# A gated feed-forward layer on one core: the start-up transposes of x from four transfers instead of two, five constant matmuls, and a weight load of its own

## The chip, the core and the metric

The kernel runs on one core of one Trainium2 chip. A core has a matrix engine (PE, with its weight loads shown apart as PEld), a vector engine (DVE), an activation engine (ACT), a general engine (POOL) and a sync engine (SP); SP and ACT also issue the transfers (DMAs) here, each on a queue of its own, and 16 DMA engines serve both. Every engine runs its own stream of instructions in order, and semaphores tie the streams together. The metric is the time of one execution in device microseconds; several runs of a kernel give a median.

## What is computed

```python
B, S, D, F = 32, 32, 1024, 3584
# x: (B, S, D), w_gate and w_up: (D, F), w_down: (F, D), all bf16
def reference(x, w_gate, w_up, w_down):
    return (_gelu(x @ w_gate) * (x @ w_up)) @ w_down
```

`_gelu` is the tanh approximation. The 32 x 32 tokens are one axis of 1024.

## The kernel before

All of the program is recorded first and emitted afterwards. `pr.add` (line 52) notes an operation with its engine, its output and its inputs; from the tiles that it reads and writes it finds the earlier operations that it must wait for. PE's stream is emitted in the order in which the program text adds the operations. The streams of the other engines are sorted by a due time `at` that is written beside each operation, and by the order of adding where due times agree. `emit` (line 106) puts the waits in front of an operation, and it is the line (117, where the instruction is made) that the profile shows for nearly all instructions; so the rows of the profile are told apart by tiles and shapes.

The tokens are two halves of 512. The first half against the first ten column blocks of the gate and up weights is multiplied in bf16, directly ("raw"); the rest of the first product and the second product use sums of operands (a Strassen-like scheme) in a 32-bit format. The change is in the first microseconds alone, and what matters of the kernel is its start:

- The tile `one` is a constant of ones. Line 200 issues eight matmuls on it, six of 512 and two of 128 columns, into PSUM bank 3. Nothing reads their result.
- The raw products need x transposed, with the contraction axis on the partitions: `xT[0]`, or `x0`, of shape (128, 8, 512), one slice for each 128 columns of x. Slices 2 to 7 come by transposing DMAs (line 215, five issues on SP). Slices 0 and 1 (`NX = 2`) are made by PE: the first 512 tokens' first 256 columns are loaded as they lie in memory into `xn` (128 tokens on the partitions, four token tiles `t`, 256 columns). Token tiles 0 and 1 come with one DMA on SP's queue, 2 and 3 with one on ACT's (line 205), 128 KB each.
- Both DMAs are the first on their queues. Behind them, SP issues four weight loads (gate, 128 KB each) and the transposing DMAs; ACT issues eight weight loads (lines 210 to 218), then loads its activation table and runs a one-element activation into `warm` (line 219). The loads go to `quad[q][:, j, k]`: four column blocks `q` of 512 columns, `j` 0 for gate and 1 for up, and row block `k`.
- Eight transposes on PE (lines 220 to 225) take a 128 x 128 piece each of `xn` with `ident`, an identity that POOL makes. For each slice `k` and each pair of token tiles `i`, two transposes fill a half-bank, and one DVE copy takes it to `xT[0]`. The banks are 6 and 7 for slice 0, and 4 and 5 for slice 1. The order is slice 0 with token tiles 0, 1, 2, 3, then slice 1 likewise.
- The raw matmuls (lines 262 to 267) follow: slice `k`, then matrix `j`, then column block `m`, into bank `2 * m + j`. The first needs both copies of slice 0 and the first gate load. Then come those of the second quad (lines 274 to 287): slices 0 to 5 in the same order, then the last two slices for each column block. The second quad's weights of row blocks 4 to 7 are four ACT loads with due times 9 and 10 (lines 268 to 270), behind ACT's first copies out of PSUM.

In a plain matmul the program gives the stationary operand and the moving operand in one call, and the instruction pair "load weights, multiply" is made of it. `held_matmul` (line 172) makes a multiply alone, on weights that stand in the array already:

```python
        def held_matmul(eng, out, lhsT, rhs, start, stop, skip_group_check=False):
            return eng.add_instruction(mybir.InstMatmult(
                start_tensor_calc=start, stop_tensor_calc=stop, ldweights=False,
```

Of the kernel before, what the change touches and what calls it, by code (L numbers as in the profile page):

```python
# [6 lines left out]
P = 128  # L7
BF16 = mybir.dt.bfloat16
# [115 lines left out]
def bass_standalone__geglu_ffn__sampling_kernel(  # L124
# [10 lines left out]
    _, F = w_gate.shape  # L135
    DK, FM = D // P, F // P
# [3 lines left out]
    x_r = xf.rearrange("(tc p) d -> p tc d", p=P)  # L140
# [3 lines left out]
    pr = _Program()  # L144

    with ExitStack() as es:
        def sb(name, shape, dtype):
            return es.enter_context(nc.sbuf_tensor(name, shape, dtype))
# [7 lines left out]
        ident = sb("ident", [P, P], BF16)  # L156
        warm = sb("warm", [P, 2], FP32)
        p1 = sb("p1", [P, 512], FP32)
        ps = es.enter_context(nc.psum_tensor("ps", [P, 8, 512], FP32))
        const0 = nc.const_aps.tensor(0.0, [P, 1], FP32)  # L160

        xT = [arena[:, a:a + 4096].rearrange("p (k n) -> p k n", n=512) for a in (16384, 0)]
        quad = [arena[:, a:a + 8192].rearrange("p (j k c) -> p j k c", j=2, k=DK) for a in (20480, 8192)]
        def duo(a): return arena[:, a:a + 4096].rearrange("p (j k c) -> p j k c", j=2, k=DK)
        wd = [[arena[:, a:a + 7168].rearrange("p (k n) -> p k n", n=512) for a in row] for row in ((0, 7168), (14336, 21504))]
        xn = hT[:, FM - 1, :].rearrange("p (t c) -> p t c", c=2 * P)
# [12 lines left out]
        def mm(bank, lhsT, rhs, start, stop, held=False, add=False):  # L179
            return pr.add("pe", held_matmul if held else "matmul", ps[:, bank, 0:rhs.shape[-1]], lhsT, rhs,  # L180
                          start=start, stop=stop, skip_group_check=add)
# [4 lines left out]
        def act(out, a, f, at):  # L186
            return pr.add("act", "activation", out, a, f, at=at)

        def dma(eng, out, a, at, name, after=()):
            return pr.add(eng, "dma_start", out, a, at=at, dma=name, after=after)  # L190
# [6 lines left out]
        pr.add("pool", "memset", ident[:, :], 0.0)  # L197
        pr.add("pool", "affine_select", ident[:, :], ident[:, :], [[-1, P]], ALU.not_equal, 1.0,
               base=0, channel_multiplier=1)
        for n in [512] * 6 + [P] * 2:  # L200
            mm(3, one[:, 0:P], one[:, 0:n], True, True)

        NX = 2
        for i, eng in enumerate(("sp", "act")):
            dma(eng, xn[:, 2 * i:2 * i + 2, :], x_r[:, 2 * i:2 * i + 2, 0:NX * P], 0, f"xn{i}")

        def load_quad(eng, q, j, k0, k1, at=0, after=()):
            dma(eng, quad[q][:, j, k0:k1, :], w_r[j][:, k0:k1, 4 * q * P:4 * (q + 1) * P], at, f"w{q}_{j}_{k0}", after)
# [8 lines left out]
            for j in range(2):  # L217
                load_quad("act", 1, j, k, k + 1)
        act(warm[:, 0:1], const0, GELU, 0)
        for k in range(NX):  # L220
            for i, b in enumerate((6, 7) if k == 0 else (4, 5)):
                half = ps[:, b, 0:P].bitcast(BF16)
                for t in range(2):
                    pr.add("pe", "transpose", half[:, t * P:(t + 1) * P], xn[:, 2 * i + t, k * P:(k + 1) * P], ident[:, :])
                pr.add("dve", "tensor_copy", xT[0][:, k, i * 256:(i + 1) * 256], half)

# [15 lines left out]
        bank = lambda b: ps[:, b, :]  # L244
# [7 lines left out]
        x0, x1 = xT  # L252

        def raw(m, j, k, b, start):
            return mm(b, quad[m // 4][:, j, k, m % 4 * P:(m % 4 + 1) * P], x0[:, k, :], start, k in (NX - 1, 3, DK - 1), add=not start and k >= NX)

        def raw_done(m, b, at):
            act(tmp[:, m % 4, :], bank(b), GELU, at)
# [3 lines left out]
        for k in range(NX):  # L262
            for j in range(2):
                for m in range(4):
                    raw(m, j, k, 2 * m + j, k == 0)
                    if k == NX - 1:
                        copy(("act", "dve")[m % 2], kept[m][:, j, :], bank(2 * m + j), 6.5 + 0.9 * j + 0.1 * m)
# [9 lines left out]
        for m, j, k in steps:  # L277
            if j is None:
                raw_done(4 + m, 2 * m, 19.4 + m * 0.87)
                continue  # L280
            begin_late = raw(4 + m, j, k, 2 * m + j, k == 0)
            if k == 3:
                copy(("act", "dve")[m % 2], kept[4 + m][:, j, :], bank(2 * m + j), 14.5)
            if k == 2 and m == j == 0:
                for k0 in range(NX, DK, 2):
                    for i in range(2):
                        load_quad("sp", 0, i, k0, k0 + 2, 9, [begin_late] if k0 == NX and i == 0 else ())


        for m in (0, 2):  # L290
            at = 21.9 + 2.59 * m
            four = [(n, j) for n in (m, m + 1) for j in range(2)]
            for n, j in four:
                copy(("act", "dve")[j], bank(2 * n + j), kept[n][:, j, :], at - 1.5 + 0.8 * (n - m) if m == 0 else at - 2)
            for k0, k1 in ((NX, 4), (4, DK)):
                for n, j in four:
                    for k in range(k0, k1):
                        raw(n, j, k, 2 * n + j, False)
                    if k1 == 4:
                        copy("act", kept[n][:, j, :], bank(2 * n + j), at + 0.6 + 0.43 * (2 * (n - m) + j))  # L300
                    elif j == 1:
                        raw_done(n, 2 * n, at + 2.7 + 1.73 * (n - m))
# [344 lines left out]
```

## Time and profile before

| | us |
|---|---|
| median of 3 runs | 272.19 |
| lowest and highest of them | 271.77, 272.44 |
| span of the profiled execution | 270.8 |
| PE busy in it | 268.2 |
| DVE, ACT, POOL busy in it | 208.2, 136.1, 37.1 |

The span goes from the first to the last instruction of one profiled execution; the time of a run contains some 1.4 us more. Times in the profile are counted from the start of the span. "Issue to landing" of a DMA is the time from its issue on a queue to the last update of its semaphore. The rows of SPq and ACTq are the issues of DMAs, which don't count as busy time of these engines. In the groups and timelines a row reads: start, length, engine, line, operation, out<-in, shape, how many, and in brackets the idle time of the engine before it with what ended it. Issues at the start, by these rows: x on both queues at 0.73 and 0.74 (0.49 and 0.46 us each), weights from 1.25 on, about one each 0.5 us on either queue, the transposing DMAs from 3.17 to 11.51 on SP; the activation table from 5.25 on ACT, for 1.28 us; the first copy out of PSUM on ACT at 7.73.

### The profile page before, as it was taken

What the parts mean: (1) busy time and instruction counts of PE and PEld (TensorE: products, weight loads), DVE (VectorE), ACT (ScalarE), POOL (GpSimd) and SP (SyncE); (2) the same over time, 40 slices, a digit from 0 to 9 for tenths busy, and PEclk for the clock granted to TensorE, in tenths of its full rate; (3) what the DMA queues carried; (4) which work ended last, traced back from release to release, by engine and by line L of the source; (5) the groups of instructions that cost most, each with busy time, mean ns of one, the idle gap of its engine ahead of it and who ended that gap; (6) DMA issues with size and microseconds to landing.
All of it is one profiled execution on the core that took longest, in us unless ns stands there. A gap on an engine that the chain in (4) does not pass through costs nothing.

```text
span 270.8 us, 3333 instructions
## 1 busy us (share of the span) xinstructions
PE 268.2 (99%) x1206; PEld 192.6 (71%) x1206; DVE 208.2 (77%) x246; ACT 136.1 (50%) x221; POOL 37.1 (14%) x23
## 2 busy tenths in 40 slices
PE   8999999999999999999999999999999999999997
PEld 4444448888888888888776776674458888888884
DVE  1338998998899889988764739379976999999921
ACT  2339877566756675667455554531220305057452
POOL 1000003123302330233344160000000000000000
DMA  6999970050492002971900070294010000002102
GB/s 205 205 316 204 280 188 4 13 141 0 116 291 60 0 0 80 254 251 51 263 0 0 0 247 27 65 351 129 0 39 19 4 0 0 0 0 80 58 21 97
DMA packets 45024, 27.47 MB, mean 101 GB/s; under 512 B 8656, under 2 KB 45008, under 8 KB 45008
## 3 DMA queue, kind: packets, MB, share of 16 engines
q1 hardware_dynamic: 42496, 25.04, 34.0%
q10 hardware_dynamic: 2512, 2.23, 3.3%
q8 instruction: 9, 0.15, 0.2%
q14 instruction: 7, 0.06, 0.1%
HBM read 23.33 MB, written 2.10 MB: 94 GB/s over the span
## 4 chain that ended last, share of the span: by engine, by line
PE 99%; DVE 0%; issue 0%
PE ps L117 99%; DVE o L117 0%
## 5 line engine op out<-in xcount | busy, mean ns | idle before, releaser
L117 PE MATMUL ps<-S,T 128*128 128x512 f32 x560 | 129.2, 391 | 0.0
L117 PEld LDWEIGHTS ps<-S,T 128*128 128x128 f32 x560 | 105.2, 188 | 22.3
L117 ACT ACTIVATE tmp<-ps 128x512 f32<-128x512 f32 x64 | 38.0, 596 | 51.7 <-PE ps L117 51.5
L117 POOL TENSOR_TENSOR T<-arena 128x1024 fp32r<-128x1024 bf16 x17 | 36.4, 2153 | 124.5 <-PE ps L117 81.7
L117 PE MATMUL ps<-T,S 128*128 128x512 f32 x224 | 51.3, 390 | 0.0
L117 DVE TENSOR_TENSOR T<-arena,T 128x1024 fp32r<-128x1024 bf16 x42 | 51.0, 1220 | 0.2
L117 PEld LDWEIGHTS ps<-T,S 128*128 128x128 f32 x224 | 42.1, 188 | 8.8
L117 ACT ACTIVATE ps<-ps 128x512 f32<-128x512 f32 x44 | 25.6, 584 | 37.0 <-PE ps L117 37.0
L117 DVE TENSOR_TENSOR hT<-tmp,ps 128x512 bf16<-128x512 f32 x56 | 37.0, 684 | 8.7 <-PE ps L117 6.7
L117 PE MATMUL ps<-arena 128*128 128x512 bf16 x192 | 43.5, 385 | 0.1
L117 DVE TENSOR_TENSOR tmp<-ps,tmp 128x512 f32<-128x512 f32 x28 | 19.4, 692 | 23.5 <-PE ps L117 23.5
L117 PEld LDWEIGHTS ps<-arena 128*128 128x128 bf16 x192 | 18.5, 99 | 23.7 <-issue 2.4
L117 DVE TENSOR_TENSOR T<-arena 128x1024 fp32r<-128x1024 bf16 x25 | 30.0, 1222 | 4.4 <-PE ps L117 4.3
L117 DVE TENSOR_TENSOR ps<-ps,tmp 128x512 f32<-128x512 f32 x32 | 22.3, 696 | 3.0 <-PE ps L117 3.0
L117 PE MATMUL ps<-arena,hT 128*128 128x512 bf16 (+2 forms) x126 | 24.6, 356 | 0.0
L117 PEld LDWEIGHTS ps<-arena,hT 128*128 128x128 bf16 x126 | 11.7, 98 | 12.7 <-issue 0.5
L117 ACT ACTIVATE tmp<-tmp 128x512 f32<-128x512 f32 x28 | 17.6, 632 | 2.4 <-DVE tmp L117 2.1
L117 ACT ACTIVATE ps<-hT 128x512 f32<-128x512 f32 x22 | 13.0, 599 | 7.6 <-DVE hT L117 7.6
L117 DVE TENSOR_TENSOR S<-hT 128x1024 fp32r<-128x1024 bf16 x14 | 16.6, 1221 | 0.0
L117 ACT ACTIVATE T<-arena 128x1024 fp32r<-128x1024 bf16 x14 | 14.8, 1059 | 0.0
L117 ACT ACTIVATE hT<-ps 128x512 f32<-128x512 f32 x18 | 9.5, 602 | 7.0 <-PE ps L117 7.0
L117 PE MATMUL ps<-S 128*128 128x512 f32 x56 | 12.9, 389 | 0.0
(33 smaller groups left out, 94.4 us busy)
## 6 DMA issues: line engine op xcount, KB each, us to landing
arena<-in_w_down_dram SPq DMA_DIRECT2D x4, 1792.0 KB, 9.4
arena<-in_w_gate_dram SPq DMA_DIRECT2D x10, 512.0 KB, 4.8
arena<-in_w_up_dram SPq DMA_DIRECT2D x10, 512.0 KB, 5.9
out_dram<-arena SPq DMA_DIRECT2D x12, 128.0 KB, 1.7
arena<-in_w_up_dram ACTq DMA_DIRECT2D x6, 128.0 KB, 5.6
arena<-in_w_gate_dram SPq DMA_DIRECT2D x3, 256.0 KB, 6.3
arena<-in_w_up_dram SPq DMA_DIRECT2D x3, 256.0 KB, 6.5
arena<-in_w_gate_dram SPq DMA_DIRECT2D x4, 128.0 KB, 5.1
```

Of the source, the lines that this page charges most:

```text
L117: ins = name(eng, *args, **kw) if callable(name) else getattr(eng, name)(*args, **kw)
```

## The change

x's first columns come as four DMAs of one token tile each: tiles 0 and 1 on SP's queue, 2 and 3 on ACT's, each with a semaphore of its own. The eight transposes run in another order, mixed between slices, with a DVE copy as soon as the second transpose of a half-bank is added; banks and copies are the same. Of the eight constant matmuls, five of 512 columns remain. The weights of the first raw matmul are loaded by an instruction of their own, which waits only for the first gate load; the matmul behind it is a held one, which waits for the copies. All other instructions keep their order on every engine.

```diff
-        for n in [512] * 6 + [P] * 2:
+        for n in [512] * 5:
             mm(3, one[:, 0:P], one[:, 0:n], True, True)
 
         NX = 2
         for i, eng in enumerate(("sp", "act")):
-            dma(eng, xn[:, 2 * i:2 * i + 2, :], x_r[:, 2 * i:2 * i + 2, 0:NX * P], 0, f"xn{i}")
+            for t in range(2 * i, 2 * i + 2):
+                dma(eng, xn[:, t, :], x_r[:, t, 0:NX * P], 0, f"xn{t}")
...
-        for k in range(NX):
-            for i, b in enumerate((6, 7) if k == 0 else (4, 5)):
-                half = ps[:, b, 0:P].bitcast(BF16)
-                for t in range(2):
-                    pr.add("pe", "transpose", half[:, t * P:(t + 1) * P], xn[:, 2 * i + t, k * P:(k + 1) * P], ident[:, :])
-                pr.add("dve", "tensor_copy", xT[0][:, k, i * 256:(i + 1) * 256], half)
+        half = {(k, i): ps[:, 6 - 2 * k + i, 0:P].bitcast(BF16) for k in range(NX) for i in range(2)}
+        for t, k in ((0, 0), (0, 1), (2, 0), (1, 0), (2, 1), (3, 0), (1, 1), (3, 1)):
+            i = t // 2
+            pr.add("pe", "transpose", half[k, i][:, t % 2 * P:(t % 2 + 1) * P], xn[:, t, k * P:(k + 1) * P], ident[:, :])
+            if t % 2:
+                pr.add("dve", "tensor_copy", xT[0][:, k, i * 256:(i + 1) * 256], half[k, i])
...
         def raw(m, j, k, b, start):
-            return mm(b, quad[m // 4][:, j, k, m % 4 * P:(m % 4 + 1) * P], x0[:, k, :], start, k in (NX - 1, 3, DK - 1), add=not start and k >= NX)
+            first = (m, j, k) == (0, 0, 0)
+            if first:
+                pr.add("pe", lambda eng, _, w: eng.ldweights(w), bank(b), quad[0][:, 0, 0, 0:P])
+            return mm(b, quad[m // 4][:, j, k, m % 4 * P:(m % 4 + 1) * P], x0[:, k, :], start, k in (NX - 1, 3, DK - 1), held=first, add=not start and k >= NX)
```

In the order of the transposes the first number is the token tile and the second the slice, so (3, 0), the sixth, is the last that slice 0 needs.

## The prediction

> **What bounds the kernel now.** I read the page's busy times first, then the chain of waits in order of time, and then, for its first pieces, the timeline of the matrix engine (PE) and of its weight loads (PEld). The page says that PE is the bound; the chain (start, length, what) says where PE is not dense.
>
> ```profile
> span 270.8 us, 3333 instructions
> PE 268.2 (99%) x1206; PEld 192.6 (71%) x1206; DVE 208.2 (77%) x246; ACT 136.1 (50%) x221; POOL 37.1 (14%) x23
> ...
> ```
>
> ```profile
> 0.73 0.04 issue
> 0.77 3.79 PE ps L117 x16
> 4.56 0.05 issue
> 4.61 264.41 PE ps L117 x1190
> ```
>
> After 4.61 us the chain is one unbroken piece of 1190 matmuls to 269.0. The only places where PE could begin sooner are the 0.77 us before its first instruction, which the change doesn't touch, and the stretch from 0.77 to 4.61, which computes nothing of the product except eight transposes. So the whole subject is 3.84 us at the start, and how the rest of the program takes a shift of its start.
>
> The timeline of PE (start, length, operation, count), and that of the weight loads, show that stretch:
>
> ```profile
> 0.77 2.93 PE L117 MATMUL ps<-const-bfloat16-1.0 128*128 128x512 bf16 x8 [0.77 <-PEq L632]
> 3.50 1.06 PE L117 MATMUL ps<-ident,hT 128*128 128x128 bf16 x8
> 4.61 2.66 PE L117 MATMUL ps<-arena 128*128 128x512 bf16 x7
> ```
>
> ```profile
> 2.86 0.15 PEld L117 LDWEIGHTS ps<-const-bfloat16-1.0 128*128 128x128 bf16 x1 [0.28 <-issue]
> 3.28 0.15 PEld L117 LDWEIGHTS ps<-const-bfloat16-1.0 128*128 128x128 bf16 x1 [0.28 <-issue]
> 3.39 0.90 PEld L117 LDWEIGHTS ps<-ident,hT 128*128 128x128 bf16 x8
> 4.58 0.14 PEld L117 LDWEIGHTS ps<-arena 128*128 128x128 bf16 x2 [0.29 <-issue]
> 4.99 0.15 PEld L117 LDWEIGHTS ps<-arena 128*128 128x128 bf16 x1 [0.28 <-DVE arena L117]
> 5.42 0.15 PEld L117 LDWEIGHTS ps<-arena 128*128 128x128 bf16 x1 [0.28 <-issue]
> 5.84 0.15 PEld L117 LDWEIGHTS ps<-arena 128*128 128x128 bf16 x1 [0.28 <-issue]
> 6.27 0.15 PEld L117 LDWEIGHTS ps<-arena 128*128 128x128 bf16 x1 [0.28 <-issue]
> 6.67 0.32 PEld L117 LDWEIGHTS ps<-arena 128*128 128x128 bf16 x2 [0.25 <-issue]
> ```
>
> Each matmul has its own weight load, so the starts of the loads are the matmuls' clock ticks. Three things are to be seen. First, the eight constant matmuls run back to back, at 0.427 us for 512 columns (2.86 to 3.28) and 0.107 for 128 (3.28 to 3.39), and the transposes follow without a pause at 3.39/3.50, also 0.107 apart ((1.06 - 0.31)/7; one takes 0.31): PE never waits for x. Second, the transposes' slots end at 3.50 + 8 x 0.107 = 4.36 and the first product's matmul is at about 4.56 to 4.61: a gap of some 0.20. Third, the first product matmuls are still 0.427 apart (4.99, 5.42, 5.84, 6.27), then 0.40, and later 0.215, which this line of the weight loads from 15 us shows ((1.82 - 0.10)/8):
>
> ```profile
> 15.09 1.82 PEld L117 LDWEIGHTS ps<-arena 128*128 128x128 bf16 x9
> ```
>
> So the array runs at half speed until about 6.64 (in the step of 0.40, 0.37 at the slow pace and the rest at the fast one), though the column of the granted clock says 1.00 there. 6.64 is 5.87 us after the first matmul.
>
> **The change, part by part.** *Constant matmuls.* One of 512 and two of 128 columns go: 0.427 + 2 x 0.107 = 0.64 us. The fifth then ends its slot at 2.86, where the sixth starts now. That is the most that can be gained in PE's start: 0.64 us.
>
> *x in four transfers.* The landings now (queue, KB, us from issue) and the copies of the transposes by the vector engine (DVE):
>
> ```profile
> hT<-in_x_dram ACTq DMA_DIRECT2D x1, 128.0 KB, 2.7
> hT<-in_x_dram SPq DMA_DIRECT2D x1, 128.0 KB, 2.5
> ```
>
> ```profile
> 3.95 0.93 DVE L117 COPY arena<-ps 128x256 bf16<-128x256 bf16 x4 [3.95 <-PE ps L117]
> ```
>
> Both x transfers are issued at 0.73/0.74 and land at 0.74 + 2.5 = 3.24 (SP) and 0.73 + 2.7 = 3.43 (ACT). The eight constants hide all of that. After the change, tiles 0 and 2 go first, 1 and 3 are issued some 0.51 later (the next issue on each queue starts at 1.25 now). The bytes are the same; in the DMA view of 1.4 to 4.4 us the engines begin to move data just before 2 and are above 300 GB/s by 2.6. So I take the last byte of x, and its landing, where they are now: 3.24 and 3.43. Bounds for the second pair: not before the first pair's earliest, which is 2.86 when nothing waits; not after a full latency from the later issue, 1.25 + 2.7 = 3.95.
>
> The chain from there: a landing or a copy reaches PE 0.12 later (the second copy starts at 3.95 + 0.21 = 4.17, takes 0.29 (so (0.93 - 0.29)/3 = 0.21 between them), the weight load follows at 4.58), a transpose runs 0.11 after its load, and its copy starts 0.35 after that (3.60 to 3.95). The transposes (0,0) and (0,1) run at 2.86 and 2.97; (1,0) at 3.24 + 0.23 = 3.47; (2,1) 3.58; (3,0) at 3.69 (tile 3 alone would allow 3.66). The first product matmul needs both copies of k=0, the second of which follows (3,0): 3.69 + 0.35 = 4.04, ends 4.33, weight load would be at 4.45. That is 0.13 sooner than 4.58. At the early bound, (3,0) at 2.86 + 5 x 0.107 = 3.39, it is 4.15 (0.43 sooner); at the late one, (3,0) at 3.95 + 0.23 = 4.18, it is 4.94 (0.36 later).
>
> *First weights on their own.* Its load no longer waits for the copy, only for the transfer: 0.03 (4.58 to 4.61), at most 0.10 (one load at the slow pace takes 0.11). It is queued after the transposes, so nothing waits behind it but its own matmul. Its transfer and that of the other matrix, both issued at 1.25:
>
> ```profile
> arena<-in_w_up_dram ACTq DMA_DIRECT2D x1, 128.0 KB, 3.3
> arena<-in_w_gate_dram SPq DMA_DIRECT2D x1, 128.0 KB, 2.8
> ```
>
> The first lands at 1.25 + 2.8 = 4.05 now. Issued 0.51 later it lands between 4.05, if the full engines set it, and 4.56, if its issue does; at 4.05 it is hidden behind the copies (4.33). At 4.56 the first matmul would be at about 4.7, 0.1 late. I take 4.05 to 4.15, because x's bytes are in front of it either way. In all, PE starts 0.15 sooner (0.13 + 0.03).
>
> *What 0.15 is worth.* I take the clock to rise at a given time, not at a given matmul, since one trace cannot tell. Before 6.64 a shift of 0.15 is 0.15/0.427 = 0.35 of a matmul, worth 0.35 x 0.216 = 0.08 us afterwards. Bounds by the same half: 0.43 + 0.10 gives -0.27, 0.36 late gives +0.18.
>
> *What the two more issues move.* Every DMA behind them on SP and ACT is issued 0.5 later: on SP four weight loads and five transposing transfers (now from 3.17 to 11.51), on ACT eight weight loads and the 1.28 us table load (5.25, then 5.75; with the warm-up activation it ends at 7.25 and the first copy on ACT is at 7.73, so 0.48 of cover stays). PE has these margins: second gate row block, 1.75 + 5.0 = 6.75, wanted by the ninth matmul at 6.67 + 3 x 0.216 = 7.32, margin 0.57; the loads issued at 9.03 and 9.48,
>
> ```profile
> arena<-in_w_gate_dram ACTq DMA_DIRECT2D x1, 256.0 KB, 6.4
> arena<-in_w_up_dram ACTq DMA_DIRECT2D x1, 256.0 KB, 6.7
> ```
>
> land at 15.43 and 16.18, wanted by the 49th and 53rd matmuls at 6.67 + 43 x 0.216 = 15.96 and 16.82: 0.53 and 0.64. These two are issued behind ACT's copies, which follow PE, so they come no later by the issue; only the transposing transfers beside them could slow them. Their cost is 0 in my sum; if the whole 0.5 arrived there, 15.93 + 0.12 + 0.11 = 16.16 against 15.96, a loss of 0.20 in all instead of the gain of 0.08. The constant and register work outside the span (272.19 - 270.8 = 1.39) stays.
>
> Sum: 272.19 - 0.08 = 272.1.
>
> [...] The trace gives one sample of the clock's rise: it survived a pause of 0.20 at 4.36. With the change PE's pause before the first product grows to about 4.42 - 4.01 = 0.41 (the last transpose slot ends at 3.69 + 3 x 0.107 = 4.01), and there are some 0.3 of short waits for x between 3.07 and 3.47.
> [...]
>
> **Rivals.**
> A, slower: the clock rises late. Place: the pauses between 3.07 and 4.42, which replace constants that kept PE busy. It decides if they add up to more than the clock's control forgives; 0.20 is forgiven in this trace, 0.7 is not known. Price: if the count begins anew at 4.42 and takes the 5.87 us of this trace, the rise is at 10.29, 3.65 later, and costs 3.65 x 0.494 = 1.80; at least, it needs more than the 3.59 us of unbroken work (0.77 to 4.36) after which the clock had not risen: 8.01, 1.37 later, 0.68. I take the long one: 272.19 + 1.80 - 0.08 = 273.9. For it: the clock had not risen after 3.59 us without any pause. Against: the pause at 4.36 evidently did not restart the count, since 2.08 us of matmuls followed and it rose.
> B, the transfers are the bound: x's second pair or a later weight block comes 0.5 late and PE stands there instead: 272.19 + 0.20 = 272.4. For it: engines are full from 2.6 on, and the margins are 0.5 to 0.6. Against: full engines mean that bytes, which don't change, set the landings.
> C, the constants were the only limit and x is there: PE starts 0.53 sooner, 272.19 - 0.27 = 271.9. Against: the later issue of tiles 1 and 3.
>
> **How the numbers follow.** Forecast 0.50, A 0.28, B 0.12, C 0.10. A measurement of this kernel tells about 0.3%, 0.8 us, from no change. Forecast, B and C lie inside that by their sums; the three runs of before spread by 0.67, so I give 0.12 of their 0.72 to faster and 0.03 to slower by chance. A is slower except at its low price, where it is 0.60 and falls inside: 0.25 of its 0.28. So faster 0.12, same 0.60, slower 0.28. The likeliest case alone spans 271.7 to 272.5 (272.1 and the runs' spread); the range goes from 271.5 to 274.0, to take in A.
>
> **What would show it.** In the timeline of PE after: five constants to 2.86, transposes with pauses until about 4.0, first product matmul near 4.4; a single weight load before the last copy ends. Right if the loads are 0.427 apart until about 6.6 as now. Wrong by A if they stay so beyond 8 us; wrong by B if a gap stands in front of the ninth, 49th or 53rd matmul, or the first load is after 4.5; wrong by C if the first product matmul is before 4.2.

## The result and the profile after

The changed kernel is slower: 273.01 us median over 12 runs (271.46 to 275.56), against 271.75 over 12 of before (271.37 to 272.44). The ratio is 1.0043, with a 95% interval of 1.0025 to 1.0060. One of the 12, 275.56, lies over 1.5% above the fastest, counts as a slow run and is left out of that ratio and of what follows, though nothing here shows that it is more than a late run. Of the other eleven, with a median of 272.49, six lie between 271.46 and 272.49, where before lies too, and five between 273.53 and 274.53; these are called late below. So the change costs little in one part of the runs, and some 2 us in the other. Of the 1.15 us between the means (272.95 against 271.80), the five late runs, which lie 1.97 above the other six in the mean, make some 0.90 (5/11 x 1.97); the other six are 0.26 slower than before.

The profiled execution (273.53 us as a run) is one of the late ones. From the page, its first line and the busy times:

```profile
span 272.0 us, 3329 instructions
...
PE 268.8 (99%) x1203; PEld 192.2 (71%) x1203; DVE 208.1 (76%) x246; ACT 136.3 (50%) x221; POOL 37.1 (14%) x23
```

PE lost no work and has three matmuls less, and yet the span is 1.2 us longer than the 270.8 of before. The chain of waits in order of time (start, length, what) now begins outside PE:

```profile
0.74 0.40 SPq L117
...
1.20 0.44 SPq L117
...
1.68 3.08 DMA arena<-in_w_gate_dram
...
4.80 0.61 PE ps L173
5.41 264.71 PE ps L117 x1189
```

The chain runs over two issues on SP and then through the first gate load, which lands 3.08 us after its issue at 1.68, at 4.76; the first product matmul (the held one, line 173) follows at 4.80, where it was at 4.61. Behind it PE is dense to the end, as before. The weight loads of PE (PEld; one for each matmul) show the rest, with start, length, count and, in brackets, the idle time before and what ended it:

```profile
3.19 0.23 PEld L117 LDWEIGHTS ps<-ident,hT 128*128 128x128 bf16 x3 [1.03 <-DMA hT<-in_x_dram]
3.69 0.45 PEld L117 LDWEIGHTS ps<-ident,hT 128*128 128x128 bf16 x5 [0.26 <-DMA hT<-in_x_dram]
4.80 0.10 PEld L258 LDWEIGHTS <-arena 128*128 128x128 bf16 x1 [0.67 <-DMA arena<-in_w_gate_dram]
...
8.19 0.15 PEld L117 LDWEIGHTS ps<-arena 128*128 128x128 bf16 x1 [0.28 <-issue]
8.62 1.42 PEld L117 LDWEIGHTS ps<-arena 128*128 128x128 bf16 x7 [0.28 <-issue]
```

There are three pauses: until 3.19 for x's first tile, until 3.69 for tile 1, and 0.67 of idle weight loading before 4.80 for the gate load. And the steps between loads are still 0.43 at 8.19; from 8.62 on seven take 1.42, which is (1.42 - 0.10)/6 = 0.22 each. I call the time at which the pace changes the rise of the array's clock, as in the prediction: about 8.68 in this execution, 6.64 in the profile of before.

The landings of x, the first pair and then, beside the first gate load, the second (queue, KB, us from issue):

```profile
hT<-in_x_dram ACTq DMA_DIRECT2D x1, 64.0 KB, 2.2
hT<-in_x_dram SPq DMA_DIRECT2D x1, 64.0 KB, 2.4
```

```profile
arena<-in_w_gate_dram SPq DMA_DIRECT2D x1, 128.0 KB, 3.1
hT<-in_x_dram ACTq DMA_DIRECT2D x1, 64.0 KB, 2.3
hT<-in_x_dram SPq DMA_DIRECT2D x1, 64.0 KB, 2.4
```

Issued at 0.73, 0.74, 1.16 and 1.20, the four transfers land at 2.95, 3.15, 3.45 and 3.65. A transfer of half the size lands only 0.1 to 0.5 sooner after its issue (2.2 and 2.4 against 2.7 and 2.5), and the second pair (3.45 and 3.65) lands no sooner than the old transfers did in the profile of before (3.43 and 3.24).

### The profile page after: what moved, and what is told of

Read it like the earlier page. It is cut to its first block, busy times and chain, and to the rows that moved or that the text cites. A ratio compares the mean times of both kernels' runs of the same rounds, so it can differ in the third digit from the quotient of the medians.

```text
span 272.0 us, 3329 instructions
## 1 busy us (share of the span) xinstructions
PE 268.8 (99%) x1203; PEld 192.2 (71%) x1203; DVE 208.1 (76%) x246; ACT 136.3 (50%) x221; POOL 37.1 (14%) x23
## 4 chain that ended last, share of the span: by engine, by line
PE 98%; DMA 1%; SPq 0%; DVE 0%; issue 0%
PE ps L117 97%; DMA arena<-in_w_gate_dram 1%; SPq L117 0%; PE ps L173 0%; DVE o L117 0%
```

## The experiments

Theory A below is that the clock rises late because PE pauses in the first microseconds; theory B, that the four transfers and the later issues cost the time; theory A', that the clock's rise needs an amount of work, whenever it is done. Two numbers of a profile turned out to tell its run's whole time: the start s of the first product matmul, and the time r at which the clock rises. If the clock is up when the product starts, the run is s and all that follows at full speed. If it is not, each microsecond between s and r does only 0.216/0.427 of the work, so 0.494 of it is lost. The constant is from the profile of the kernel with its own first load (e4), where the loads of the product are 0.22 apart from the first on:

```profile
4.37 0.15 PEld L257 LDWEIGHTS <-arena 128*128 128x128 bf16 x1
4.64 1.40 PEld L117 LDWEIGHTS ps<-arena 128*128 128x128 bf16 x7
```

Its run took 271.44 with s = 4.64, which leaves 266.8. So a run should take 266.8 + s + 0.494 x (r - s):

| profile of | s | r | by the sum | its run |
|---|---|---|---|---|
| before | 4.61 | 6.64 | 272.4 | 272.4 (see below) |
| after | 4.80 | 8.68 | 273.5 | 273.53 |
| e1, eight constants in the changed kernel | 4.73 | 5.45 | 271.9 | 271.90 |
| e2, before with five constants | 4.61 | 6.36 | 272.3 | 272.25 |
| e3, changed kernel with a filling | 5.18 | 5.18 or before | 272.0 | 271.99 |
| e5, changed kernel with eight constants and the filling | 5.57 | 6.78 | 273.0 | 272.95 |
| e6, before with a filling | 4.59 | 4.59 or before | 271.4 | 271.39 |
| e7, before without constants | 4.71 | 9.30 | 273.8 | 273.74 |
| e8, before with six constants | 4.83 | 5.75 | 272.1 | 272.01 |
| e10, before with a filling and the own load | 4.83 | 6.79 | 272.6 | 272.54 |
| e11, before with five constants and a half | 4.71 | 5.28 | 271.8 | 271.76 |
| e12, before with five constants, again | 4.85 | 9.02 | 273.7 | 273.64 |

All agree within 0.1. The profile of before isn't tied to one of its runs; the other profiles' runs take 1.53 to 1.55 more than their spans (not the 1.4 that I took from before's median), and 270.84 + 1.54 gives its 272.4. The rule was written down, in the expectation of e12, before e9 to e12 ran, so e10, e11 and e12 test it. The profile of e9 has a stall behind s, and is read below. So in these profiles what a kernel's start costs is in s, in r, or in a stall, and the experiments can be sorted by these. Medians of the experiments stand against the median of before on the same chip, 271.76 for e1 to e4, 271.89 for e5 to e8 and 271.77 for e9 to e11.

**e1: the changed kernel with its constants back.**

```diff
-        for n in [512] * 5:
+        for n in [512] * 6 + [P] * 2:
```

> The changed kernel with the eight constant matmuls of before. Theory A (the clock rises late because PE pauses in the first microseconds): the constants cover PE to 3.5 us, one pause of about 0.4 before the first product matmul is left; the clock rises near 6.6 as before and the time is 271.7 to 272.1, with a spread of about 1 us. Rival B (the four transfers and the queues moved by 0.5 cost the time): it stays at 272.7 to 273.3.

Measured: 272.24 (271.71 to 274.43, 11 runs), ratio 1.0029 (1.0009 to 1.0049). Nine runs end at 272.59 or before, two at 274.27 and 274.43. It is between the two expectations: the constants remove most late runs, but not all, and the median of the other nine, 272.05, is still above before's. That points to two causes. The chain of its profile (271.90 as a run) shows, in front of the first product matmul:

```profile
4.17 0.52 DVE arena L117 x2
4.69 0.04 issue
4.73 0.58 PE ps L173
```

It goes through the two copies of slice 0, not through the gate load, which landed at 4.63. The last transpose that slice 0 needs is the sixth in the new order and the fourth in the old one; where x is in time, as here, the second copy ends at 4.69 instead of before's 4.46. So the new order can cost a start of its own. No run has it alone.

**e2: before with five constants.** No transfer, no order and no load is changed.

```diff
-        for n in [512] * 6 + [P] * 2:
+        for n in [512] * 5:
```

> The kernel before with five constant matmuls and nothing else changed. PE pauses from 2.86 to 3.4, when x lands. Theory A: the clock rises late in most runs, 272.6 to 273.6, spread over 2 us. Rival B: the constants were idle filling, so the time is that of before, 271.5 to 271.9.

Measured: 273.41 (272.19 to 273.98, 8 runs), ratio 1.0052 (1.0033 to 1.0070). The pause alone, between the last constant's end at 2.86 and the first transpose, does about as much harm as the whole change (1.0043). Theory B can't explain it, since the transfers are those of before. Its profile is of one of the two early runs (272.25):

```profile
3.50 0.80 PEld L117 LDWEIGHTS ps<-ident,hT 128*128 128x128 bf16 x8 [1.34 <-DMA hT<-in_x_dram]
...
5.85 0.15 PEld L117 LDWEIGHTS ps<-arena 128*128 128x128 bf16 x1 [0.28 <-issue]
6.28 3.81 PEld L117 LDWEIGHTS ps<-arena 128*128 128x128 bf16 x18 [0.28 <-issue]
```

The pause was 0.64 there, and the clock rose at 6.36 all the same. A late run of this kernel is shown in e12.

**e3: the changed kernel with a filling between transposes and product.**

```diff
+        for n in [512]:
+            mm(3, one[:, 0:P], one[:, 0:n], True, True)
```

> The changed kernel with one more constant matmul of 512 columns (0.43 us) between the last transpose and the first product matmul, where PE pauses from 4.2 to 4.76. Theory A: of the 1.1 us of pauses 0.4 go, so the time falls from 273.0 to 271.8 to 272.5, and the clock rises sooner than 8.6 in the profile. Rival B: the first product matmul is where it was or 0.1 later, 273.0 to 273.2.

Measured: 273.14 (271.86 to 274.91, 12 runs), ratio 1.0048 (1.0023 to 1.0072). This expectation of theory A failed: the median did not fall. But the runs fall apart into six at 271.86 to 272.38 and six at 273.90 to 274.91, with nothing between. The one profile is of an early run (271.99). In it x came early (the first tile at 2.85), so that the pauses among the transposes were 0.04 and 0.12; the first product matmul came only at 5.18, 0.93 behind the filling's end at 4.25, and the clock was up by then. So the filling left a pause of 0.9, but in this run that pause did no harm, and why the other six are late no profile shows.

**e4: before with the first weights loaded on their own.** The edit is the last part of the change's diff, alone.

> The kernel before with the first weights loaded on their own and nothing else changed. Both theories: first product matmul 0.03 to 0.10 sooner, worth half of that; 271.6 to 271.9, no difference that can be measured.

Measured: 271.85 (271.44 to 272.44, 12 runs), ratio 1.0004 (0.9994 to 1.0014). The own load does nothing that can be seen, for or against; the interval allows a change of up to 0.14%.

**e5: the changed kernel with eight constants and the filling.** The edits of e1 and e3 together.

> The changed kernel with eight constants before the transposes and one of 512 columns after them, so that PE has next to no pause from 0.77 us on. [...] Theory B (the four transfers delay the first weights, hence the start by 0.1 to 0.3): the median is 0.1 to 0.3 above that of the next kernel, e6, whose transfers are the old ones. [...]

Measured: 272.41 (271.90 to 272.95, 12 runs), ratio 1.0021 (1.0012 to 1.0030). No run is above 273: PE has next to no pause, and none is late, as theory A has it. What is left of the loss, some 0.5 us, is put down to theory B by the one profile, of the slowest run (272.95):

```profile
1.68 3.84 DMA arena<-in_w_gate_dram
5.52 0.05 issue
5.57 0.61 PE ps L173
```

The gate load, issued at 1.68, landed at 5.52, and the product began at 5.57. The size of B was expected too small: the distance to e6 is 0.93 (272.41 - 271.48), not 0.1 to 0.3, as the gate load can come later than the one profile of after had shown.

**e6: before with a filling of 256 columns.**

```diff
+        for n in [256]:
+            mm(3, one[:, 0:P], one[:, 0:n], True, True)
```

> The kernel before with one constant matmul of 256 columns (0.21 us at the slow pace) between the last transpose and the first product matmul, where PE pauses for 0.20. Theory A: before has no late runs, so little is to be had; 271.6 to 271.8, none above 272.6. If the pause of 0.20 had a price of its own, the median falls by 0.2 or more.

Measured: 271.48 (271.36 to 272.27, 11 runs), ratio 0.9988 (0.9978 to 0.9997). The median is 0.4 below before's 271.89. By the expectation that is the sign of a price of the 0.20 pause; but e10 below holds the same filling and does not repeat it, so that stays open. The profile shows more. Its transposes are these:

```profile
3.39 0.73 PEld L117 LDWEIGHTS ps<-ident,hT 128*128 128x128 bf16 x8
```

In before the same eight took 0.90. Here their steps go from 0.107 to 0.056 within them: the clock rose at about 3.89. Up to then PE had done the same as in before, matmul for matmul within 0.01 us, and there the clock rose at 6.64. So the same work brought the rise 3.12 us after the first matmul in one execution and not in the other, where it came after 5.87.

**e7: before without constants.**

```diff
-        for n in [512] * 6 + [P] * 2:
-            mm(3, one[:, 0:P], one[:, 0:n], True, True)
```

> The kernel before without constant matmuls: PE begins with the transposes at 3.5 us. Theory A (work before a pause counts for nothing): as slow as the kernel with five constants and old transfers (273.4) or up to 0.5 faster or slower, since the rise is then counted from 3.5: 272.8 to 273.8. Rival A' (the rise needs an amount of work since the start, so many constants fewer cost in proportion): three constants cost 1.65 there (0.64 us of work), so eight would cost several times that, above 275.

Measured: 273.01 (272.67 to 273.74, 6 runs), ratio 1.0045 (1.0031 to 1.0060). With no constants the kernel is as slow as the changed one and not slower than e2 with five. So A' falls (it had this run above 275): it isn't the amount of work that counts here. By the median (273.01 with none, 273.41 with five), the five constants before a pause of 0.6 or more are worth nothing; but two of e2's eight runs (272.19 and 272.25) are faster than all six here, and in the profile of the second the clock rose 2.86 after the first transpose, so in those runs it did count. The profile's r of 9.30 is 5.87 after the first transpose's weight load at 3.43. That this is the same figure as in before, from its first constant matmul to 6.64, may be chance, since r scatters between runs (in e6 it is 3.12), but the delay agrees with a start that counts from 3.43.

**e8: before with six constants.**

```diff
-        for n in [512] * 6 + [P] * 2:
+        for n in [512] * 6:
```

> The kernel before with six constants of 512 columns and without the two of 128: 0.21 us of work less, and a pause of about 0.2 at most before the transposes. Theory A: a pause of that length is forgiven, as the one at 4.36 is; 271.6 to 272.0 and no run above 273. Rival A': a third of what five cost, 0.5 slower, 272.2 to 272.4. If even 0.2 more of pause is too much, some runs lie at 273.3 to 274.3.

Measured: 271.60 (271.46 to 272.10, 11 runs), ratio 0.9994 (0.9985 to 1.0003). One constant of 0.43 us more than e2, and no run is late. In its profile x came late, and PE paused from 3.28 to 3.73 and again before 4.83; the clock rose at 5.75 all the same. Pauses of 0.44 and 0.26 were forgiven there.

**e9: before with one tiny transfer more on each queue.**

```diff
+            dma(eng, o11[0:1, 0, i * P:(i + 1) * P], x_r[0:1, 0, i * P:(i + 1) * P], 0, f"tiny{i}")
```

> The kernel before with one tiny transfer (one partition, 256 bytes, into a scratch place) behind x on each of the two queues, so that the first weights are issued 0.4 to 0.5 later and nothing else is changed: two transfers of x, eight constants. Theory B1 (the first weights land late because they are issued behind one more transfer): the first gate load lands at 4.5 to 4.8 in the profile and the first product matmul is at 4.6 to 4.9; time 271.9 to 272.2. Theory B2 (the later issue is covered by the full DMA engines, and it is the cutting of x that makes the weights late): the load lands at 4.0 to 4.3 as in the kernels with two transfers, and the time is 271.6 to 271.9.

Measured: 272.34 (271.95 to 273.32, 12 runs), ratio 1.0023 (1.0012 to 1.0035). The chain of its profile:

```profile
1.92 4.30 DMA arena<-in_w_up_dram
6.22 0.04 issue
6.26 262.58 PE ps L117 x1186
```

B1 is right that it costs time (a transfer of 256 bytes ahead of the weights on each queue costs 0.57 at the median, as much as e5 shows; the median is 0.14 over its range), but wrong about the place in this profile: here the gate load landed at 4.21, where B2 had it, and the product began at 4.55; it was the first up load, issued on ACT at 1.92, that landed 4.30 later, and the fifth matmul waited for it until 6.26. The clock was up, so that stall of 1.07 - 0.22 = 0.85 counts in full: 266.8 + 4.55 + 0.85 = 272.2, and the run took 272.27. Since x is not cut in this kernel and the order of the transposes is the old one, the later issue alone is enough for a loss of the size of the second part. That the cutting or the new order has a price beside it is not shown, nor excluded.

**e10: before with the filling and the own load.** The edits of e6 and e4 together.

> The kernel before with 256 more constant columns behind the transposes, and the first weights loaded on their own: the parts that cost nothing, without the four transfers and with no pause. Expected 271.4 to 271.7, 0.0 to 0.2 per cent faster than before, no run above 272.4.

Measured: 271.70 (271.34 to 272.54, 12 runs), ratio 0.9999 (0.9987 to 1.0011). No difference; the median is at the upper end of what was expected, and two runs (272.49 and 272.54) lie above the 272.4 that was to be the highest. Whether the filling of e6 gains 0.1% stays open; no version was found that is surely faster than before.

**e11: before with five constants and a half.**

```diff
-        for n in [512] * 6 + [P] * 2:
+        for n in [512] * 5 + [2 * P]:
```

> The kernel before with five constants of 512 columns and one of 256: the pause before the transposes is 0.43 us with x at 3.5, between six constants (no late run in 11) and five (six of eight at 272.9 and more). [...] Rival A' (the amount of work counts): every run is the same 0.4 later or so, 272.1 to 272.5.

Measured: 272.00 (271.67 to 274.01, 12 runs), ratio 1.0022 (1.0003 to 1.0041). Eight runs are at 272.42 or below, one at 272.78, three at 273.48 to 274.01: a part of the runs is late, and it is not the even shift of A'. In its profile, of an early run (271.76), the pause before the transposes was 0.56 and the clock rose at 5.28. So the number of late runs follows the length of the constants: none of 11 with six, three or four of 12 with half a one less, six of 8 (272.92 and more) with five.

**e12: before with five constants, a second profile.** The kernel is that of e2.

> Another look at the kernel before with five constants, for the time of the clock's rise in a run that is late. Over nine profiles so far, the run's time is 266.8 + s + 0.494 x (r - s) within 0.1, where s is the start of the first product matmul and r the rise of the clock. Theory A: a run of 273.2 to 274 has r at 8.2 to 9.8 with s at 4.6 to 4.8. If such a run has r below 7, the lost time lies elsewhere.

Measured: 273.64. The loads of PE:

```profile
3.76 0.77 PEld L117 LDWEIGHTS ps<-ident,hT 128*128 128x128 bf16 x8 [1.61 <-DMA hT<-in_x_dram]
4.82 0.14 PEld L117 LDWEIGHTS ps<-arena 128*128 128x128 bf16 x2 [0.28 <-issue]
...
8.65 0.15 PEld L117 LDWEIGHTS ps<-arena 128*128 128x128 bf16 x1 [0.28 <-issue]
9.05 2.04 PEld L117 LDWEIGHTS ps<-arena 128*128 128x128 bf16 x10 [0.25 <-issue]
```

x landed at 3.72, so the pause lasted from 2.86 to 3.76, 0.90 where e2's early run had 0.64. Then PE worked on with one small pause, and the step from 8.65 to 9.05 was still 0.40: r is 9.02, s 4.85, and the sum 273.7. In the late runs with a profile, this one, that of after and that of e7, the lost time is a late clock.

## Why the prediction was wrong

The forecast was 272.1, a shift of -0.08, called no difference; measured is +0.43%. The range held the median, and rival A, to which I gave 0.28, is the larger part of what happened. The step that failed is "I take the clock to rise at a given time": it put the new pauses at nothing in the sum, and in a part of the runs they move the rise by 2 us and more. The second is the bound on the first weights' landing. In the profile of after, both signs that I had named are there: steps of 0.427 beyond 8 us (A), and the first load after 4.5 (B). By the steps:

- *Constant matmuls.* Right: the fifth ends its slot at 2.86, and this is all that is saved. It was no gain, since x isn't there.
- *x in four transfers.* Half wrong. The first transposes were to run at 2.86 and 2.97 on the assumption that the first pair has landed by then; it landed at 2.95 and 3.15, and they ran at 3.19. For the second pair I took 3.24 and 3.43, the landings of before, because the bytes are the same; they came at 3.65 and 3.45. The sixth transpose ran at 3.88 (3.69 predicted). The second pair lies within the bounds that I had written down (2.86 to 3.95); for the first pair I had given none. One profile was a poor measure here: over all profiles the second pair of small transfers lands at 3.23 to 3.68 (four profiles) and the two large ones at 3.19 to 3.95 (ten). The order of the transposes I took for free; e1 shows that it need not be.
- *First weights on their own.* Here a bound failed. "I take 4.05 to 4.15, because x's bytes are in front of it either way", and 4.56 as the latest: the load landed at 4.76 in the profile of after, 4.63 in e1, 5.14 in e3 and 5.52 in e5, against 4.03 to 4.38 in the nine profiles with two transfers and no further one ahead of the weights. The busy engines did not hide the later issue; in e9, with one more issue and x in two transfers, it was the up load that came late, at 6.22 against 4.44 to 4.69 in the same nine. With s at 4.80 instead of 4.45, PE started later, not sooner. The load as an instruction costs and gains nothing that can be seen (e4).
- *What a shift is worth.* The half price is right: 0.494 of what lies between s and r is what all profiles show. But "I take the clock to rise at a given time" is the step that decided, and it failed: r was 8.68 instead of 6.64, and (8.68 - 6.64) x 0.494 = 1.01 of the 1.11 that the sum finds between the two profiles; the later s gives the other (4.80 - 4.61) x 0.506 = 0.10.
- *The two more issues.* I put them at nothing, and rival B at 0.20 for weights wanted by the ninth, 49th or 53rd matmul. The profile of after has no gap there, so these margins held. The cost was in front, at the first loads, and larger: 0.52 at the median in e5 and 0.57 in e9.
- *Rival A.* It is right that the pauses make the clock late, and where. Its price, 1.80 with the rise 3.65 later, was the case of a count that begins anew; late runs are about 2 above the others, but that this comes so near is partly luck: in the profile of after the rise is 2.04 later than in that of before, and costs 1.01. What I had not thought of is that it strikes a part of the runs. I had one profile and took its rise for a constant of the kernel; over four profiles with eight constants and old transfers, e4, e6, e10 and before, r lies anywhere from 3.89 to 6.79. So the median of a kernel with late runs falls between the groups or in one of them by the number of late runs, at 273.0 over all 12 here and not at 273.9. Its deciding point, "0.20 is forgiven, 0.7 is not known", has no sharp answer: a pause of 0.44 before the transposes in e8's profile, 0.56 in e11's and 0.64 in e2's was forgiven, 0.90 in e12's was not, and the share of late runs grows between six constants and five. Whether a run is late by its own pause or by something else is not told apart; that something beside PE's work plays a part, e6 beside before shows (3.89 and 6.64 after the same work).

The time r moves between profiles whose PE had done the same work (3.89 in e6 and 6.64 in before), and between runs of one kernel (6.36 and 9.02 with five constants). The two groups of e3 lie 2.1 apart (medians 271.96 and 274.03).

What stays open: why the first loads land so much later for an issue that is 0.4 later (issue to landing grew from 2.8 to 3.1 in after, and to 3.8 in e5), whether four transfers as such add to it, and what the new order of the transposes costs by itself. What sets r in a run is not shown either; its values in the profiles go from 3.89 (e6) to 9.30 (e7).

## What to carry to other kernels

Filling work at the start, meant to bring the array's clock up, should last until the real work comes: here, with the old transfers, eight and six constants left no run late (none above 272.54 and 272.10), and five, with a pause of 0.64 us and more behind them in two profiles, were worth no more at the median than none (273.41 and 273.01). When a transfer on the starting path is cut in two, one cost to count is the later issue of what stands behind it on the queue (0.57 us at the median in e9, for a transfer of 256 bytes on each queue). And when times fall into two groups, look first for what differs between a run of each, and only then at the median: here s and r of one profile tell the run's time within 0.1 us.

## What was not expected of the hardware

- The clock's rise moves by nearly 3 us between executions with eight constants and old transfers: 3.89 us from the start in e6 (a run of 271.39), before 4.65 in e4 (271.44), 6.64 in before, 6.79 in e10 (272.54). By the sum that is enough for the whole scatter of before's runs, 271.3 to 272.5; but before itself has one profile, so this is argued.
- The profile's own column of the granted clock says 1.00 throughout, in executions where matmuls of one shape follow each other at 0.43 us up to r and at 0.22 after it.
- x's transfers, unchanged in code and first on their queues, landed at 3.19 (e6) to 3.73 us (e10) on SP and 3.37 to 3.95 on ACT in kernels with two transfers. The eight constants, which end at 3.50, cover only the early ones.
